# Softmax sums of a pooled-attention and feed-forward kernel: from a trip through DRAM to block transposes on VectorE

## The chip, the cores and the metric

The kernel runs on one core of a Trainium2 chip. The metric is the device time of one execution in microseconds, the median of several runs. TensorE (PE) does the products, VectorE (DVE) and ScalarE (ACT) the elementwise work, GpSimd (POOL) the reductions over partitions, and SyncE (SP) issues most of the transfers; SP's issues run in their program order, so one that waits holds up those behind it.

## The reference

```python
def _attn_ref(q, k, v):                       # 8 batches, 8 heads, 576 positions, 64 wide
    k_p = k.reshape(B, H, Sp, pool, D).mean(axis=3)      # pool 8: 72 keys
    v_p = v.reshape(B, H, Sp, pool, D).mean(axis=3)
    scores = scale * np.matmul(q, k_p.transpose(0, 1, 3, 2))
    scores = scores - np.max(scores, axis=-1, keepdims=True)
    attn = np.exp(scores)
    attn = attn / (np.sum(attn, axis=-1, keepdims=True) + 1e-09)
    return np.matmul(attn, v_p)
...
x = attn_out.transpose(0, 2, 1, 3).reshape(4608, 512)
h = np.maximum(x @ w_in, 0.0)                 # d_ff 2048
out = h * h @ w_out
```

The two weight matrices come as float64 and are turned to float32 on the chip.

## The kernel before

The 4608 tokens go in nine chunks (c) of 512. Of each chunk, 16 steps (fc) each make 128 of the 2048 hidden columns; step s = 16c + fc. `hidden` makes h with TensorE, ScalarE takes relu and square (r), `split_hidden` splits the result into a high part gh (ScalarE) and a rest gl (VectorE), and `project`, three steps later (LAG), multiplies both with the output weights w_o into four accumulators o: twelve products gh, gl, gh per step. In chunks 0 and 1 the products are plain (PLAIN = 2); from chunk 2 on `seven` makes two steps' h from seven products of half size per pair of steps, with sums of weight quarters (S1 to S4, tiles w_S) and of token halves (T1 to T4, B11 to B22, tiles x_T and x_B). An even step of it holds on VectorE the additions u, h, h (`soon`, behind a copy u by ScalarE) and one more h (`then`, behind another such copy). `x_sums` and `x_operand` make the x_T and x_B from xf: a subtraction xf, a copy by ScalarE for the high part, and a subtraction x_T or x_B on VectorE for the rest. T2 is the operand of the second product of a chunk.

The attention that a chunk needs is made in the steps ahead of it, by head pair (p = 0 to 3). For chunks from 2 on: `transpose_q` (qs, st), `scores` (sps on TensorE, sc on ScalarE, their maximum mx over partitions on GpSimd), `exponents` (ScalarE, and the sums tot over partitions on GpSimd, every row of tot the same), then the sums' reciprocals, and `weigh_values` (product av, times rb into xf on VectorE). Before, the sums went through DRAM: `send_sums` writes one row of each tot (rs), `fetch_sums` reads it as 128 x 8 (rc), `reciprocals` works on that (rr) and writes it (rd), and `fetch_reciprocals` reads it back, broadcast over 64 partitions (rb). A pair's first step is 16c - 23, -19, -15 or -11; the offsets of its stages from there stand in STEADY.

The order of all work is written out: a loop over the steps records each step's instructions, and a table `work`, filled by `at(step, f, ...)`, says which function is recorded in which step; inside a step the loop takes the kinds in a fixed order. Each engine then works through its instructions in that order. The output weights are turned to float32 in chunk 0 and 1, kept in DRAM, and fetched anew for each step (`fetch_weights`, w_o<-kept, 512 KB) into one of 40 buffers (SLOTS) that they share with the weights, x and xf tiles. k and v are summed in groups by transfers that add, issued by GpSimd (k<-in_k_dram). A weight is turned to float32 by `magnitude` (two activations on ScalarE, wf and raw) and `to_float32` (three operations on VectorE).

The tiles mx and tot share three buffers, rb, rr and qs have one, and the products sps, av, kps and pps share two PSUM buffers.

Of the kernel before, what the change touches and what calls it, by code (L numbers as in the profile page):

```python
# [37 lines left out]
def pooled_attn_relu2_ffn(  # L38
# [43 lines left out]

    STEADY = ((-23, -19, -15, -11), (-1, 1, 3, 5, 6, 6, 7, 8))
    EARLY = ((-13, -12, -9, -8), (0, 1, 2, 3, 4))
# [9 lines left out]
    kept = ctx.enter_context(tc.tile_pool(name="kept", bufs=1, space=bass.MemoryType.DRAM))  # L94
    dram = ctx.enter_context(tc.tile_pool(name="dram", bufs=3, space=bass.MemoryType.DRAM))
    ps_o = ctx.enter_context(tc.tile_pool(name="ps_o", bufs=1, space=bass.MemoryType.PSUM))
# [59 lines left out]

    def to_float32(*keys):
        parts = []
        for key in keys:
            words, m = raw.pop(key).rearrange("p a (n w) -> p a n w", w=2), wf[key]  # L160
            parts.append((words, m, m.bitcast(U32)))
        for _, m, _ in parts:
            DVE.tensor_scalar(m, m, EXP_MIN, EXP_MAX, op0=ALU.max, op1=ALU.min)
        for words, _, m in parts:
            DVE.scalar_tensor_tensor(m, m, 3, words[..., 0], op0=ALU.logical_shift_left, op1=ALU.bitwise_or)
        for words, _, m in parts:
            DVE.scalar_tensor_tensor(m, words[..., 1], 0x80000000, m, op0=ALU.bitwise_and, op1=ALU.bitwise_or)
# [235 lines left out]

    PER = 2 * CH // P

    def send_sums(c, p):
        sc, tots = live.pop((c, p))
        rs = dram.tile([2, CH], F32, name=f"rs_{c}_{p}", tag="rs")
        for i in range(2):
            dma(rs[i:i + 1], tots[i][0:1])  # L410
        live[c, p] = (sc, rs)

    def fetch_sums(c, p):
        sc, rs = live.pop((c, p))
        rc = sb.tile([P, PER], F32, name=f"rc_{c}_{p}", tag="rc", bufs=2)
        dma(rc, rs.rearrange("o (a f) -> (o a) f", f=PER))
        live[c, p] = (sc, rc)

    def reciprocals(c, p):
        sc, rc = live.pop((c, p))  # L420
        rr = sb.tile([P, PER], F32, name=f"rr_{c}_{p}", tag="rr", bufs=1)
        DVE.tensor_scalar(rr, rc, 1e-9, float(POOL), op0=ALU.add, op1=ALU.mult)
        DVE.reciprocal(rr, rr)
        rd = dram.tile([2, CH], F32, name=f"rd_{c}_{p}", tag="rd")
        dma(rd.rearrange("i (a f) -> (i a) f", f=PER), rr)
        live[c, p] = (sc, rd)

    def fetch_reciprocals(c, p):
        sc, rd = live.pop((c, p))
        rb = sb.tile([P, CH], F32, name=f"rb_{c}_{p}", tag="rb", bufs=1)  # L430
        for i in range(2):
            dma(rb[i * D:(i + 1) * D, :], rd[i:i + 1, :].broadcast_to([D, CH]))
        live[c, p] = (sc, rb)


# [211 lines left out]
    def project(c, fc):  # L647
# [12 lines left out]
        def store():  # L660
            for t in range(NTT):
                ob = half_tile("ob", f"ob_{c}_{t}")
                ACT.copy(ob, accs[c][t])
                rows = out[c * CH:(c + 1) * CH].rearrange("(p t) d -> t p d" if c == 0 else "(t p) d -> t p d", t=NTT)
                outs.append((rows[t], ob))
# [103 lines left out]
    weigh_values(0, 0)()  # L769
    to_float32(keys[0])  # L770
    token_turn(0, 2)()
    magnitude(keys[1])
    weigh_values(0, 1)()
    begin(0)
# [52 lines left out]
    START = {transpose_q: 9, scores: 12, exponents: 13}  # L827
    stages = (transpose_q, scores, exponents, send_sums, fetch_sums, reciprocals, fetch_reciprocals, weigh_values)
    for c in range(1, NCH):
# [10 lines left out]
        for p in range(NPAIR):  # L840
            s = c * NFC + first[p]
            at(s - 2 if c < PLAIN else max(s - QL, 8), load_q, c, p)
            for d, f in zip(offsets, names):
                at(max(s + d, START[f]) if c == PLAIN and f in START else s + d - (f is transpose_q and c >= PLAIN and p != 2), f, c, p)

# [4 lines left out]
    for s in range(-PRO, len(steps) + LAG):  # L850
        todo = work.get(s, [])
        soon, then, activate = hidden(*steps[s]) if 0 <= s < len(steps) else (None, None, None)
        later = [f(*a) for f, a in sorted(((f, a) for f, a in todo if f in on_pe), key=lambda x: x[0] is weigh_values)]
        for kind in (fetch_sums, fetch_weights):
            for f, a in todo:
                if f is kind:
                    f(*a)
        split_at(s, s - 2)
        if store:
# [17 lines left out]
        for f, a in todo:  # L877
            if f is fetch_reciprocals:
                f(*a)
        for f, a in todo:  # L880
            if f in first:
                f(*a)
        issue_loads()
        for f, a in todo:
            if f not in first + on_pe + last + (x_sums, x_operand, reciprocals, fetch_weights, fetch_sums, fetch_reciprocals, first_sums):
                f(*a)
# [48 lines left out]
```

## Time and profile before

| | us |
|---|---|
| median of 3 runs (lowest, highest) | 916.34 (914.07, 920.58) |
| profiled execution | 919.03 |
| its span | 917.3 |
| granted clock of TensorE, mean | 0.996 |
| busy: TensorE, VectorE, ScalarE, GpSimd | 897.3, 578.6, 511.2, 419.0 |

A row of a timeline has the start, the time and the engine of a run of like instructions (xN of them), and in brackets the idle time of the engine before the first and what ended it. A row of the groups has the busy time in all, and the mean of one in ns. A row of the waits has who waited for whom, the time in all, how many times, and the longest. A row of a table by stretches has the stretch, its length, the busy time of PE, PEld, DVE, ACT and POOL with the number of instructions in brackets, the granted clock as a share of the full one, the DMA engines' share and GB/s.

### The profile page before, as it was taken

How to read it: one execution, taken by the hardware profiler on the slowest of the kernel's cores; microseconds unless marked ns; L12 is line 12 of the kernel's file. 1: busy time of each engine (PE TensorE's matmuls, PEld its weight loads, DVE VectorE, ACT ScalarE, POOL GpSimd, SP SyncE). 2: the span in 40 equal slices, each digit the busy share in tenths (PEclk: the TensorE clock that was granted, in tenths of full speed). 3: DMA queues.
4: the chain of work that ended last, by engine and by line, in shares of the span. 5: the costliest groups of instructions: out<-in, count | busy, mean ns of one | idle time of the engine just before them, and what ended most of it. 6: DMA issues, size and time to landing. Idle time of an engine off the chain costs nothing.

```text
span 917.3 us, 14127 instructions
## 1 busy us (share of the span) xinstructions
PE 897.3 (98%) x5090; PEld 716.4 (78%) x5093; DVE 578.6 (63%) x941; ACT 511.2 (56%) x1018; POOL 419.0 (46%) x227
## 2 busy tenths in 40 slices
PE   8999999999999999999899999999999999999998
PEld 4344445677778888888788888888888888889987
DVE  7997679767788878666746485658544653353221
ACT  5776656656566655554654556545654564344343
POOL 4754136456655555556545656665444444200000
PEclk9999999999999999999999999999999999999999
DMA  9897564777556655766565557553534353345401
GB/s 222 252 266 189 136 149 114 227 216 203 144 134 165 142 141 139 174 145 140 111 174 147 134 130 188 140 137 99 184 100 123 100 168 111 127 142 202 185 1 47
DMA packets 157335, 138.72 MB, mean 151 GB/s; under 512 B 94488, under 2 KB 122136, under 8 KB 157264
## 3 DMA queue, kind: packets, MB, share of 16 engines
q1 hardware_dynamic: 128464, 127.13, 46.2%
q0 software_dynamic: 28800, 10.68, 10.2%
q8 instruction: 40, 0.66, 0.3%
q14 instruction: 31, 0.25, 0.1%
HBM read 119.65 MB, written 18.06 MB: 150 GB/s over the span
## 4 chain that ended last, share of the span: by engine, by line
PE 68%; DVE 10%; DMA 8%; issue 5%; ACT 4%; POOL 3%; SPq 1%; DVEq 0%; ACTq 0%; POOLq 0%
PE o L34 33%; PE h L34 30%; DMA w_o<-kept 3%; PE av L34 2%; PE sps L34 2%; DVE gl L34 1%; DVE wf_i L34 1%; DMA k<-in_k_dram 1%; DVE xf L34 1%; POOL tot L34 1%; ACT sc L34 1%; DMA rb<-rd 1%; DMA raw_i<-in_moe_w_in_dram 1%; POOL v L34 1%; ACT r L34 1%
## 5 line engine op out<-in xcount | busy, mean ns | idle before, releaser
L34 PE MATMUL o<-w_o,gh 128*128 128x512 f32 x1024 | 323.2, 397 | 4.4 <-DMA w_o<-kept 4.2
L34 POOL PARTITION_ALL_REDUCE tot<-sc x56 | 190.0, 3442 | 85.4 <-issue 81.2
L34 PEld LDWEIGHTS o<-w_o,gh 128*128 128x128 f32 x1024 | 185.0, 189 | 49.6 <-issue 6.3
L34 PE MATMUL o<-w_o,gl 128*128 128x512 f32 x512 | 201.5, 393 | 0.0
L34 ACT ACTIVATE r<-h 128x512 f32<-128x512 f32 x144 | 83.4, 594 | 91.2 <-PE h L34 74.0
L34 PE MATMUL h<-x_T,w_S 128*128 128x256 f32 x1008 | 130.4, 283 | 0.7 <-ACT x_T L34 0.4
L34 POOL PARTITION_ALL_REDUCE mx<-sc x56 | 109.9, 2002 | 40.3 <-ACT sc L34 29.1
L34 PEld LDWEIGHTS h<-x_T,w_S 128*128 128x128 f32 x1008 | 124.9, 190 | 1.1 <-ACT x_T L34 0.6
L34 PEld LDWEIGHTS o<-w_o,gl 128*128 128x128 f32 x512 | 96.5, 188 | 21.2 <-DVE gl L34 0.2
L34 DVE TENSOR_TENSOR h<-h,u 128x256 f32<-128x256 f32 x168 | 72.7, 433 | 60.1 <-ACT u L34 31.8
L34 ACT COPY u<-h 128x256 f32<-128x256 f32 x112 | 41.7, 372 | 121.9 <-PE h L34 75.1
L34 PE MATMUL h<-x_B,w_A 128*128 128x256 f32 x672 | 98.6, 283 | 0.5 <-ACT r L34 0.5
L34 DVE TENSOR_TENSOR gl<-r,gh 128x512 fp32r<-128x512 f32 x128 | 93.4, 765 | 6.0 <-ACT gh L34 5.9
L34 POOL DMA_DIRECT2D v<-in_v_dram x36 | 44.0, 1222 | 115.5 <-issue 39.6
L34 PEld LDWEIGHTS h<-x_B,w_A 128*128 128x128 f32 x672 | 91.7, 189 | 5.6 <-ACT r L34 0.9
L34 POOL DMA_DIRECT2D k<-in_k_dram x36 | 44.1, 1225 | 110.0 <-issue 53.0
L34 DVE TENSOR_TENSOR u<-h,u 128x256 f32<-128x256 f32 x56 | 23.3, 417 | 105.4 <-ACT u L34 105.3
L34 ACT ACTIVATE r<-r 128x512 f32<-128x512 f32 x144 | 84.2, 625 | 1.1
L34 DVE TENSOR_TENSOR st<-qs,st 64x512 fp32r<-64x512 f32 x56 | 46.3, 827 | 56.9 <-ACT st L34 56.0
L34 ACT CAST gh<-r 128x512 fp32r<-128x512 f32 x128 | 79.0, 617 | 0.9 <-PE o L34 0.7
L34 ACT ACTIVATE sc<-sc 72x512 f32<-72x512 f32 x56 | 34.5, 632 | 69.4 <-DVE sc L34 69.3
L34 PE MATMUL o<-wf_o,r 128*128 128x512 f32 x128 | 59.8, 611 | 0.0
(95 smaller groups left out, 1220.3 us busy)
## 6 DMA issues: line engine op xcount, KB each, us to landing
w_o<-kept SPq DMA_DIRECT2D x128, 512.0 KB
out_dram<-ob SPq DMA_DIRECT2D x36, 256.0 KB
raw_i<-in_moe_w_in_dram SPq DMA_DIRECT2D x16, 512.0 KB
raw_o<-in_moe_w_out_dram SPq DMA_DIRECT2D x16, 512.0 KB
kept<-w_o SPq DMA_DIRECT2D x16, 512.0 KB
rb<-rd SPq DMA_DIRECT2D x56, 128.0 KB
k<-in_k_dram POOLq DMA_DIRECT2D x36, 144.0 KB, 5.3
v<-in_v_dram POOLq DMA_DIRECT2D x36, 144.0 KB, 5.2
```

The costliest lines, as they stand in the source:

```text
L34: return lambda *a, **k: self.tc.keep_in_program_order(f(*a, **k))
```

## The change

1. `send_sums`, `fetch_sums` and `fetch_reciprocals` go. `turn_first` and `turn_second` transpose one tot each (64 x 512, in blocks of 32 x 32) into the halves of rb, so that each block's first column holds 32 tokens' sums; `reciprocals` works on those columns (128 x 16) into rr and transposes rr, broadcast along the block's columns, back into rb, where every row of a block then holds the reciprocals. `weigh_values` stays 8 steps behind a pair's first step.
2. In a step, turn_first is recorded ahead of `soon`, turn_second behind it, and reciprocals ahead of `x_sums` and `x_operand`.
3. From step 49 on a step's fetch of output weights is recorded at the end of the step before.
4. In the head, the first block of input weights is turned to float32 in two halves with `token_turn` recorded between, and the x_1 copy stands ahead of the next `magnitude`.
5. The first pair of chunk 1 is transposed a step earlier.
6. In a step, `token_normalise` and `late_turn_k` are recorded ahead of the other work of their group.
7. Two of the last chunk's four output copies are made by VectorE.

```diff
-    STEADY = ((-23, -19, -15, -11), (-1, 1, 3, 5, 6, 6, 7, 8))
+    STEADY = ((-23, -19, -15, -11), (-1, 1, 3, 5, 5, 5, 8))
...
-    def to_float32(*keys):
+    def to_float32(*keys, rows=slice(0, 2)):
...
-            words, m = raw.pop(key).rearrange("p a (n w) -> p a n w", w=2), wf[key]
+            words, m = raw[key].rearrange("p a (n w) -> p a n w", w=2)[:, rows], wf[key][:, rows]
...
+    def turn_first(c, p):
+
+        sc, tots = live[c, p]
+        rb = sb.tile([P, CH], F32, name=f"rb_{c}_{p}", tag="rb", bufs=1)
+        DVE.transpose(rb[:D, :], tots[0][:D, :])
+        live[c, p] = (sc, rb, tots[1])
+
+    def turn_second(c, p):
+        sc, rb, tot = live[c, p]
+        DVE.transpose(rb[D:, :], tot[:D, :])
+        live[c, p] = (sc, rb)
 
     def reciprocals(c, p):
...
+        rr = sb.tile([P, CH // SQ, 1], F32, name=f"rr_{c}_{p}", tag="rr", bufs=1)
+        DVE.tensor_scalar(rr, rb.rearrange("p (t w) -> p t w", w=SQ)[:, :, :1], 1e-9, float(POOL), op0=ALU.add, op1=ALU.mult)
         DVE.reciprocal(rr, rr)
...
+        DVE.transpose(rb.rearrange("p (t w) -> p t w", w=SQ), rr.broadcast_to([P, CH // SQ, SQ]))
...
-                ACT.copy(ob, accs[c][t])
+                (DVE.tensor_copy if c == NCH - 1 and t % 2 else ACT.copy)(ob, accs[c][t])
...
-    to_float32(keys[0])
+    to_float32(keys[0], rows=slice(0, 1))
     token_turn(0, 2)()
+    to_float32(keys[0], rows=slice(1, 2))
+    weigh_values(0, 1)()
     magnitude(keys[1])
-    weigh_values(0, 1)()
...
-                at(max(s + d, START[f]) if c == PLAIN and f in START else s + d - (f is transpose_q and c >= PLAIN and p != 2), f, c, p)
+                at(max(s + d, START[f]) if c == PLAIN and f in START else s + d - (f is transpose_q and (p != 2 if c >= PLAIN else p == 0)), f, c, p)
...
-        for kind in (fetch_sums, fetch_weights):
+        if s <= (PLAIN + 1) * NFC:
             for f, a in todo:
-                if f is kind:
+                if f is fetch_weights:
                     f(*a)
+        for f, a in todo:
+            if f is turn_first:
+                f(*a)
         split_at(s, s - 2)
...
         split_at(s, s - 1)
+        for f, a in todo:
+            if f is turn_second:
+                f(*a)
         for f in later:
             f()
...
+        for f, a in sorted(todo, key=lambda x: x[0] not in (token_normalise, late_turn_k)):
...
+        for f, a in work.get(s + 1, []):
+            if f is fetch_weights and s >= (PLAIN + 1) * NFC:
+                f(*a)
         while summed:
             summed.pop(0)()
-        for kind in (x_sums, x_operand, reciprocals, sum_of_quarters, first_sums):
+        for kind in (reciprocals, x_sums, x_operand, sum_of_quarters, first_sums):
```

On VectorE, in front of chunk 3 (steps 46 and 47; the first number behind a name is the pair or the hidden column block, the last one a running number), before:

```order
L34 TENSOR_TENSOR u_2_14_3228<-h_14_3202,u_2_14_3228 128x256
L34 TENSOR_TENSOR h_15_3203<-h_15_3203,u_2_14_3228 128x256
L34 TENSOR_TENSOR h_14_3202<-h_15_3203,u_2_14_3228 128x256
L34 TENSOR_TENSOR h_15_3203<-h_15_3203,u_2_14_3229 128x256
L34 TENSOR_TENSOR gl_12_3243<-r_12_3189,gh_12_3242 128x512
L34 TENSOR_TENSOR gl_13_3262<-r_13_3191,gh_13_3261 128x512
L34 TENSOR_TENSOR vp_2645<-v_4_1_2734 72x256
L34 TENSOR_TENSOR x_B_3280<-xf_1_2910,x_B_3280 128x512
L34 TENSOR_TENSOR x_T_3283<-xf_0_2336,x_T_3283 128x512
L34 TENSOR_TENSOR x_T_3286<-xf_0_2336,x_T_3286 128x512
L34 TENSOR_TENSOR xf_1_2910<-xf_1_2910,xf_0_2336 128x2x256
L34 TENSOR_TENSOR x_T_3333<-xf_1_2910,x_T_3333 128x512
```

With the change, step 46 first up to its second transpose (the xf of x_sums stands ahead of both extracts):

```order
L34 STREAM_TRANSPOSE rb_0_3195<-tot_0_0_3099 64x512
L34 TENSOR_TENSOR u_2_14_3181<-h_14_3155,u_2_14_3181 128x256
L34 TENSOR_TENSOR h_15_3156<-h_15_3156,u_2_14_3181 128x256
L34 TENSOR_TENSOR h_14_3155<-h_15_3156,u_2_14_3181 128x256
L34 STREAM_TRANSPOSE rb_0_3195<-tot_0_1_3100 64x512
```

and from there to the x_T of T2:

```order
L34 TENSOR_TENSOR h_15_3156<-h_15_3156,u_2_14_3182 128x256
L34 TENSOR_TENSOR gl_12_3198<-r_12_3142,gh_12_3197 128x512
L34 TENSOR_TENSOR gl_13_3217<-r_13_3144,gh_13_3216 128x512
L34 TENSOR_TENSOR vp_2610<-v_4_1_2703 72x256
L34 TENSOR_SCALAR rr_0_3233<-rb_0_3195 128x16
L34 RECIPROCAL rr_0_3233<-rr_0_3233 128x16
L34 STREAM_TRANSPOSE rb_0_3195<-rr_0_3233 128x512
L34 TENSOR_TENSOR x_B_3237<-xf_1_2869,x_B_3237 128x512
L34 TENSOR_TENSOR x_T_3240<-xf_0_2307,x_T_3240 128x512
L34 TENSOR_TENSOR x_T_3243<-xf_0_2307,x_T_3243 128x512
L34 TENSOR_TENSOR xf_1_2869<-xf_1_2869,xf_0_2307 128x2x256
L34 TENSOR_TENSOR x_T_3288<-xf_1_2869,x_T_3288 128x512
```

rb_0 is of pair 0 of chunk 4, which is turned while chunk 2 ends. Its first transpose moved in ahead of u and its second ahead of the last h, and the two small operations and the transpose back stand ahead of x_B, so that the x_T of T2 (the last row of each) stands five instructions further back; rr stood behind the x_T of T4 before.

In SP's queue, from the fetch for step 63 to that for step 65 (w_o_14 is that of chunk 3; rs_0 to rb_0 are of pair 0 of chunk 5), before:

```order
L34 DMA w_o_12_4314<-kept_1724 128x1024
L34 DMA rs_0_4351<-tot_0_0_4220 1x512
L34 DMA rs_0_4351<-tot_0_1_4221 1x512
L34 DMA k_6_1_4363<-in_k_dram 72x4x128
L34 DMA rc_0_4383<-rs_0_4351 128x8
L34 DMA w_o_13_4385<-kept_1809 128x1024
L34 DMA rd_0_4420<-rr_0_4417 128x8
L34 DMA w_o_14_4450<-kept_1866 128x1024
L34 DMA rb_0_4478<-rd_0_4420 64x512 x2
```

And with the change:

```order
L34 DMA w_o_12_4200<-kept_1715 128x1024
L34 DMA k_6_0_4205<-in_k_dram 72x4x128
L34 DMA w_o_13_4283<-kept_1792 128x1024
L34 DMA k_6_1_4298<-in_k_dram 72x4x128
L34 DMA w_o_14_4337<-kept_1849 128x1024
L34 DMA q_3_4404<-in_q_dram 32x10x32 x4
L34 DMA q_3_4404<-in_q_dram 32x6x32 x4
```

The transfers rs, rc, rd and rb are gone from between the fetches, and w_o_14 stands behind w_o_13 and a load of k with nothing of the softmax ahead of it.

On ScalarE, step 9 of chunk 0, the activations behind r_9, before:

```order
L34 ACTIVATE r_9_958<-r_9_958 128x512
L34 ACTIVATE wf_o_824<-raw_o_827 128x512
L34 ACTIVATE raw_o_827<-raw_o_827 128x512
L34 ACTIVATE wf_o_965<-raw_o_828 128x512
L34 ACTIVATE raw_o_828<-raw_o_828 128x512
L34 ACTIVATE kh_978<-kps_0_973 64x4x72 x4
```

And with the change:

```order
L34 ACTIVATE r_9_959<-r_9_959 128x512
L34 ACTIVATE kh_973<-kps_0_968 64x4x72 x4
L34 ACTIVATE wf_o_825<-raw_o_828 128x512
L34 ACTIVATE raw_o_828<-raw_o_828 128x512
L34 ACTIVATE wf_o_985<-raw_o_829 128x512
L34 ACTIVATE raw_o_829<-raw_o_829 128x512
```

The four kh, which the kl on VectorE take in, moved ahead of the four activations of two output weights.

More of the change, by code (lines that the diff above doesn't have):

```diff
@@ L94, in pooled_attn_relu2_ffn @@
     kept = ctx.enter_context(tc.tile_pool(name="kept", bufs=1, space=bass.MemoryType.DRAM))
-    dram = ctx.enter_context(tc.tile_pool(name="dram", bufs=3, space=bass.MemoryType.DRAM))
     ps_o = ctx.enter_context(tc.tile_pool(name="ps_o", bufs=1, space=bass.MemoryType.PSUM))
@@ L155, in magnitude @@
         ACT.activation(words[..., 0], halves[..., 1], AF.Copy, scale=LOW)
-    def to_float32(*keys):
+    def to_float32(*keys, rows=slice(0, 2)):
         parts = []
         for key in keys:
-            words, m = raw.pop(key).rearrange("p a (n w) -> p a n w", w=2), wf[key]
+            words, m = raw[key].rearrange("p a (n w) -> p a n w", w=2)[:, rows], wf[key][:, rows]
             parts.append((words, m, m.bitcast(U32)))
+            if rows.stop == 2:
+                raw.pop(key)
         for _, m, _ in parts:
@@ L401, in exponents @@
         live[c, p] = (sc, tots)
[L404 to L417, printed above, removed]
+    def turn_first(c, p):
[7 more added lines that the diff above has]
+        live[c, p] = (sc, rb)
     def reciprocals(c, p):
-        sc, rc = live.pop((c, p))
-        rr = sb.tile([P, PER], F32, name=f"rr_{c}_{p}", tag="rr", bufs=1)
-        DVE.tensor_scalar(rr, rc, 1e-9, float(POOL), op0=ALU.add, op1=ALU.mult)
+        sc, rb = live[c, p]
+        rr = sb.tile([P, CH // SQ, 1], F32, name=f"rr_{c}_{p}", tag="rr", bufs=1)
+        DVE.tensor_scalar(rr, rb.rearrange("p (t w) -> p t w", w=SQ)[:, :, :1], 1e-9, float(POOL), op0=ALU.add, op1=ALU.mult)
         DVE.reciprocal(rr, rr)
[L424 to L433, printed above, removed]
+        DVE.transpose(rb.rearrange("p (t w) -> p t w", w=SQ), rr.broadcast_to([P, CH // SQ, SQ]))
     def token_scores(c, p):
@@ L827, in pooled_attn_relu2_ffn @@
     START = {transpose_q: 9, scores: 12, exponents: 13}
-    stages = (transpose_q, scores, exponents, send_sums, fetch_sums, reciprocals, fetch_reciprocals, weigh_values)
+    stages = (transpose_q, scores, exponents, turn_first, turn_second, reciprocals, weigh_values)
     for c in range(1, NCH):
@@ L877, in pooled_attn_relu2_ffn @@
         for f, a in todo:
-            if f is fetch_reciprocals:
-                f(*a)
-        for f, a in todo:
             if f in first:
@@ L883, in pooled_attn_relu2_ffn @@
         issue_loads()
-        for f, a in todo:
-            if f not in first + on_pe + last + (x_sums, x_operand, reciprocals, fetch_weights, fetch_sums, fetch_reciprocals, first_sums):
+        for f, a in sorted(todo, key=lambda x: x[0] not in (token_normalise, late_turn_k)):
+            if f not in first + on_pe + last + (x_sums, x_operand, turn_first, turn_second, reciprocals, fetch_weights, first_sums):
                 f(*a)
```

## The prediction

> **What bounds the kernel now.** I read the page first: busy shares, then the chain that ended last.
>
> ```profile
> PE 897.3 (98%) x5090; PEld 716.4 (78%) x5093; DVE 578.6 (63%) x941; ACT 511.2 (56%) x1018; POOL 419.0 (46%) x227
> ...
> PE 68%; DVE 10%; DMA 8%; issue 5%; ACT 4%; POOL 3%; SPq 1%; DVEq 0%; ACTq 0%; POOLq 0%
> ```
>
> TensorE is busy for 897.3 of 917.3 us, and the change leaves its instructions and their order alone. So everything that can be won lies in 20 us of gaps, and everything that can be lost is a new gap. The second view is therefore what TensorE waited for.
>
> ```profile
> PE o L34 <- DMA w_o<-kept: 4.2, 4, 2.4
> PE pps L34 <- DVE kl L34: 2.1, 1, 2.1
> PE sps L34 <- DVE xf L34: 1.9, 2, 1.0
> ```
>
> Four waits on the fetched output weights (4.2 us in all, the longest 2.4) and one on VectorE's kl (2.1 us) are the largest that the change touches. Third, since the change moves work from DMA queues to VectorE, I looked for places where VectorE has nothing to spare, by stretches of 24 us.
>
> ```profile
> 240.00:264.00 24.00, 23.95 (x132) 19.92 (x131) 19.68 (x31) 11.74 (x22) 11.92 (x8) 1.00 0.49 116
> 264.00:288.00 24.00, 22.61 (x145) 19.54 (x144) 20.50 (x32) 16.95 (x34) 13.45 (x8) 1.00 0.62 171
> 288.00:312.00 24.00, 24.00 (x155) 21.12 (x154) 21.07 (x33) 13.95 (x29) 12.35 (x7) 1.00 0.58 140
> 312.00:336.00 24.00, 23.65 (x149) 20.55 (x149) 18.07 (x27) 15.95 (x31) 13.96 (x7) 1.00 0.55 129
> ```
>
> The fourth column is VectorE. In chunk 2 (256 to 333 us) it works 18 to 21 of 24 us, against 63% over the span: here, and in front of each later chunk's first product, an instruction more on VectorE can reach TensorE. Elsewhere it has some 9 us free in 24.
>
> **What the turns cost on VectorE.** Twenty-eight head pairs get three transposes, a tensor_scalar and a reciprocal each.
>
> ```profile
> L34 DVE STREAM_TRANSPOSE qs<-q 128x512 f32<-128x512 f32 x28 | 19.6, 701 | 0.0
> L34 DVE RECIPROCAL rr<-rr 128x8 f32<-128x8 f32 x28 | 5.7, 203 | 1.0
> L34 DVE TENSOR_SCALAR rr<-rc 128x8 f32<-128x8 f32 x28 | 5.0, 179 | 0.4
> L34 DVE STREAM_TRANSPOSE still<-still 128x32 f32<-128x32 f32 x1 | 0.2, 211 | 0.0
> ```
>
> The 128x512 transpose is in the trace: 0.70 us. From 0.21 us at 32 columns to 0.70 at 512 its time goes by the columns (0.49 us for 480). No row shows 64 partitions: bounded between half (0.35) and whole (0.70), I take 0.70, since the columns set the time. The two small ones grow from 8 to 16 columns and stay near 0.18 and 0.20. Sum per pair: 3 x 0.70 + 0.38 = 2.48 us, where 0.38 stood before; so +2.1 us per pair and 28 x 2.1 = +59 us on VectorE, 579 to about 638. The DMA trip that goes (rs, rc, rd, rb) was never itself what TensorE waited for, so its removal is worth only what it clears for others.
>
> GpSimd is summing the next pair while VectorE turns. Whether that stretches a transpose is open.
>
> ```profile
> L34 DVE TENSOR_TENSOR xf<-xf,xf 128x512 f32<-128x512 f32 x14 | 20.3, 1452 | 0.2
> L34 DVE TENSOR_TENSOR xf<-av,rb 128x512 f32<-128x512 f32 x28 | 19.3, 689 | 31.1 <-PE av L34 25.9 <-DMA rb<-rd 2.9 <-DMA q<-in_q_dram 1.8
> ```
>
> The form with both inputs in SBUF takes 1452 ns in the mean, the form with one in PSUM 689; the 28 transposes stay at a mean of 701. I take no stretching; a transpose stretched as the first row would add 0.75 us to each. The Trainium skill, "SBUF — State Buffer", section "Who interferes with whom", says that an operation of VectorE with at most one SBUF input does not contend with GpSimd outside the two-port modes; by that rule nothing is added, and the trace's rows agree for the 128-partition transposes, while no row shows it for the new ones. Were the rule wrong here, the sum below would be about 5 us higher.
>
> **The head (parts 4 to 6).** Three stalls are edited.
>
> ```profile
> 28.13 1.10 PE L34 MATMUL h<-x,wf_i 128*128 128x512 f32 x2 [1.44 <-ACT x L34]
> 54.14 1.07 PE L34 MATMUL sps<-kf,st 64*64 64x72 f32 x18 [1.10 <-DVE st L34]
> ...
> 94.79 0.42 DVE L34 TENSOR_TENSOR kq<-k 72x256 f32<-72x256 f32 x1 [1.93 <-DMA k<-in_k_dram]
> ...
> 101.54 0.65 ACT L34 ACTIVATE wf_o<-raw_o 128x512 f32<-128x512 f32 x1
> ...
> 105.42 1.86 DVE L34 SCALAR_TENSOR_TENSOR kl<-kps,kh 64x288 fp32r<-64x288 f32 x4 [4.51 <-ACT kh L34]
> 107.43 0.86 PE L34 MATMUL pps<-ident,te 128*72 128x128 f32 x4 [2.08 <-DVE kl L34]
> 108.00:112.00 4.00, 4.00 (x8) 1.80 (x7) 3.25 (x7) 3.86 (x7) 1.19 (x1) 0.62 0.33 37
> ```
>
> The first two stalls, 1.44 and 1.10 us, should shrink, since the first half of the weights is done before the second is begun and the transpose no longer stands behind the wf_o block. But at 94.79 VectorE waits 1.93 us for the last addition of k, whose transfers GpSimd issues, and the kps transposes at 101 hang on it: TensorE 2.5 us earlier at 54 would wait there instead. I count nothing for the first two (bound: 2.5 us, if those transfers also move up). The third counts: kh goes ahead of four activations that begin at 101.54 and last 2.2 us, so kl ends 2.2 us earlier and the idle 2.08 us goes. Behind it the granted clock was 0.62 over 4 us, worth (1 - 0.62) x 4 = 1.5 us, which I take to go with the idle. **Head: -3.6 us**, bounds -1 and -6.
>
> The Trainium skill, "TensorE: Matmul & The Clock Gate", section "What's actually happening", lets the clock halve after an idle window of about 3.4 us. By that, idle times of 2.08 us here and 2.43 us below would cost no clock, 2.9 us less would be gained, and the sum below would give 918.6. The trace does not agree: 0.62 stands right behind 2.08 us of idle, so I keep the trace's price.
>
> **The weight fetches (part 3).** In the queue of SP, fetch w_o_14 stood behind rd, which waits for VectorE's rr; now it is issued a step earlier and rd is gone.
>
> ```profile
> 448.67 0.32 SPq L34 DMA_DIRECT2D rd<-rr  x1
> 449.08 0.39 SPq L34 DMA_DIRECT2D w_o<-kept  x1
> ...
> 456.32 1.22 PE L34 MATMUL o<-w_o,gh 128*128 128x512 f32 x2 [2.43 <-DMA w_o<-kept]
> ...
> 460.51 0.88 PE L34 MATMUL h<-x_B,w_A 128*128 128x256 f32 x6
> ...
> 551.81 0.73 PE L34 MATMUL o<-w_o,gh 128*128 128x512 f32 x2 [0.59 <-DMA w_o<-kept]
> ...
> 634.00 0.62 PE L34 MATMUL o<-w_o,gh 128*128 128x512 f32 x2
> ...
> 636.75 0.88 PE L34 MATMUL h<-x_B,w_A 128*128 128x256 f32 x6
> ```
>
> At 456 TensorE idles 2.43 us, and the twelve o products behind it take 460.51 - 456.32 = 4.19 us, where a project step elsewhere takes 636.75 - 634.00 = 2.75: 1.44 us of lowered clock. With the 0.59 at 551.81 that is 4.46 us. The other two waits (4.2 - 2.43 - 0.59 = 1.2 us together) are in chunks 1 and 2, where the issue's place is unchanged or the tile's buffer comes free late; they stay. **Fetches: -4.5 us**, bounds -2 (the landing stays as slow as the 7 us here) and -5.7.
>
> **Chunk 2, where VectorE is full.** Four pairs turn there: 4 x 2.1 = 8.4 us more against 24 - 19.68, 24 - 20.50, 24 - 21.07 and 24 - 18.07, together 16.7 us free in 96. Part of the free time is the wait between two additions, which recurs in each even step:
>
> ```profile
> 345.41 0.43 DVE L34 TENSOR_TENSOR h<-h,u 128x256 f32<-128x256 f32 x1 [0.44 <-ACT u L34]
> ```
>
> turn_second now stands exactly in that 0.44 us, so 4 x 0.44 = 1.8 of the 8.4 us are covered. Of the other 6.6 some falls into stretches in which VectorE waits for TensorE, at the end of 312 to 336 above all. Bounds 0 and +6.6; I take **+2.5 us**, nearer the lower end, as TensorE in 312:336 has 23.65 of 24 us of its own work and VectorE 5.9 us free there.
>
> **Front of each chunk.** The pair that turns at step 16c - 2 puts turn_first, turn_second and the reciprocals ahead of the chain gl, vp, x_B, x_T, xf, x_T that makes T2, needed by the second product of the chunk. Three transposes from start to start about 0.62 each, 0.35 for the small ones, less the 0.44 that is covered: 1.8 us later.
>
> ```profile
> 351.31 0.69 DVE L34 TENSOR_TENSOR x_T<-xf,x_T 128x512 fp32r<-128x512 f32 x1 [0.69 <-ACT x_T L34]
> ...
> 352.05 2.30 PE L34 MATMUL h<-x_T,w_S 128*128 128x256 f32 x17 [0.34 <-DVE x_T L34]
> ...
> 444.61 0.69 DVE L34 TENSOR_TENSOR x_T<-xf,x_T 128x512 fp32r<-128x512 f32 x1 [0.99 <-ACT x_T L34]
> ...
> 445.64 1.60 PE L34 MATMUL h<-x_T,w_S 128*128 128x256 f32 x12
> ...
> 636.81 0.69 DVE L34 TENSOR_TENSOR x_T<-xf,x_T 128x512 fp32r<-128x512 f32 x1 [0.69 <-ACT x_T L34]
> ...
> 637.46 2.38 PE L34 MATMUL h<-x_T,w_S 128*128 128x256 f32 x18
> ```
>
> At chunk 3 TensorE already waits for it: +1.8. At chunk 6 x_T ends at 637.50 and is used at 637.46: no slack, +1.8. At chunk 4 it ends at 445.30 and is needed at 445.64 (0.34), and VectorE waited 0.99 there instead of 0.69 (0.30): 1.8 - 0.64 = +1.1, of which I take 0.7 as the waits ahead of it close too; the same for chunk 5, where I found the same slack. Chunks 7 and 8 have more room. **Fronts: +5.0 us**, bounds 0 and +9 (with all six at 1.5).
>
> The store's copies on VectorE (part 7) run beside the last o products: 0.
>
> **Sum**: -3.6 - 4.5 + 2.5 + 5.0 = -0.6 us. The profiled execution took 919.03 us (span 917.3), so it would be 918.4; the median of the runs is 916.34, 2.7 lower, and the same difference gives 915.7.
>
> **Rivals.** (a) The turns are hidden: fronts and chunk 2 cost at most 1 us. For it: VectorE's waits between those rows (0.99, 0.69, 0.44) can close, and 59 us stand against 339 us idle. Against: the slacks at chunks 3 and 6. Then -8.1 + 1 = -7, or down to -11 with the head's whole bound: 905 to 909. (b) Slower: the front of chunks 3 to 6 becomes VectorE-bound, and each new stall, 0.7 (0.35 + 0.34) + 1.8 = 2.5 us at chunk 3, passes the length (2.1 us) behind which the clock was lowered; four fronts at 1.8 + 1.45 = 13 and chunk 2 at +6.6, less 8.1, is +11.5: 928. It decides from stalls of about 2 us upward; for it the 2.08 and 2.43 us rows, against it that 1.44 us at 28 is shorter than that and was followed by the ordinary 1.10 for two products. (c) The wait for GpSimd takes the place of the DMA's.
>
> ```profile
> 361.67 6.86 POOL L34 PARTITION_ALL_REDUCE tot<-sc  x2
> ...
> 365.50 0.41 DVE L34 TENSOR_TENSOR u<-h,u 128x256 f32<-128x256 f32 x1
> ```
>
> Here the second tot ends at 368.53, and turn_second, estimated at 1.5 us behind u at 365.50, would wait 1.5 us, with h, gl and what follows queued behind it. TensorE needs gl two steps on, with about 2.5 us of cover, so one such wait costs nothing; were the cover 1 us, 0.6 us for each of some eight pairs, +5: 921. (d) The fetches wait for buffers rather than for rd, so part 3 does nothing: +4.5 - 0.6 = +3.9: 920.
>
> **Chances.** The forecast with (c) and (d), which stay within 1%, 0.74; (a) as far as below 907.2, 0.15; (b) above 925.5, 0.11. One per cent, 9.2 us, is about what a measurement of this kernel can tell from no change. The range runs from 907 to 923: the lower end is the sum with fronts and chunk 2 near nothing, the upper one the sum with fronts and chunk 2 at +4 more each; about a tenth is left out on either side.
>
> **What would show it.** Right: no TensorE wait on kl near 105, and clock 1.0 behind it; w_o<-kept waits of about 1.2 us; x_T waits grown from 0.7 us to 5 or so; VectorE near 638 us; transposes of 64x512 at 0.70 us. Wrong: transposes at half or twice that; long waits of VectorE on tot; TensorE waiting for h or gl in the middle of chunks; the clock row below 1.0 at chunk fronts.

## The result and the profile after

The changed kernel took 922.41 us (median of 9 runs, 919.55 to 928.57) against 919.48 us before (9 runs, 914.07 to 921.41) on the same chip: a ratio of 1.0056, 95% interval 1.0034 to 1.0078. A second comparison gave 922.54 against 920.10 us, 1.0034 (1.0008 to 1.0060). So by the ratios it is 3 to 5 us slower; the time lay inside the range, but 0.6 us less had been forecast, and the sign is wrong. The profiled execution, 928.08 us with a span of 925.9, stands at the slow end of these runs, so some of its waits may be larger than usual; a second profile of the same kernel (e4 below) took 920.19 us, span 918.0.

The page of the changed kernel, busy times and the chain that ended last:

```profile
PE 900.0 (97%) x5090; PEld 719.3 (78%) x5093; DVE 642.5 (69%) x1030; ACT 510.3 (55%) x1016; POOL 409.9 (44%) x227
...
PE 65%; DVE 12%; issue 7%; DMA 5%; ACT 4%; POOL 4%; SPq 0%; DVEq 0%; ACTq 0%; POOLq 0%
```

VectorE gained 63.9 us (578.6 to 642.5; 59 were forecast) and two points of the chain. What TensorE waited for, in the changed kernel:

```profile
PE kps L34 <- DVE tm L34: 5.8, 1, 5.8
PE sps L34 <- DVE xf L34: 3.0, 2, 1.6
PE h L34 <- ACT r L34: 2.2, 1, 2.2
PE o L34 <- DMA w_o<-kept: 1.9, 1, 1.9
...
PE h L34 <- DVE x_T L34: 1.5, 5, 0.3
...
PE h L34 <- DVE h L34: 0.7, 1, 0.7
```

The wait on kl is gone and those on w_o fell from 4.2 to 1.9 us, as forecast; new are 5.8 us for tm and 0.7 for h, and the wait for r grew from 0.5 to 2.2 us. The five waits for x_T are the fronts of the later chunks: 0.3 us each.

The groups of the new VectorE work:

```profile
L34 DVE STREAM_TRANSPOSE rb<-tot 64x512 f32<-64x512 f32 x56 | 39.3, 703 | 28.9 <-POOL tot L34 27.7
L34 DVE STREAM_TRANSPOSE rb<-rr 128x512 f32<-128x512 f32 x28 | 19.9, 711 | 1.0
L34 DVE TENSOR_SCALAR rr<-rb 128x16 f32<-128x16 f32 x28 | 9.0, 320 | 0.0
L34 DVE RECIPROCAL rr<-rr 128x16 f32<-128x16 f32 x28 | 7.1, 253 | 1.0
```

Sixty-four partitions take as long as 128 (703 and 711 ns). Per pair that is 39.3 / 28 + (19.9 + 9.0 + 7.1) / 28 = 2.69 us, where 2.48 was forecast: the two small operations took 0.32 and 0.25 us, not 0.18 and 0.20. No transpose is stretched beside GpSimd: the 84 of the pairs took 694 to 714 ns. The Trainium skill, "SBUF — State Buffer", section "Who interferes with whom", says that an operation of VectorE with at most one SBUF input, outside the two-port modes, does not contend with GpSimd, and the trace agrees for these transposes.

Where TensorE lost and won, in the timelines. At 106 us:

```profile
101.54 0.42 DVE L34 TENSOR_TENSOR kq<-k 72x256 f32<-72x256 f32 x1 [6.40 <-DMA k<-in_k_dram]
...
106.45 0.74 PE L34 MATMUL kps<-ident,kq 72*128 72x72 f32 x4 [5.81 <-DVE tm L34]
...
90.90 1.19 POOL L34 DMA_DIRECT2D k<-in_k_dram  x1 [9.05 <-issue]
95.01 1.20 POOL L34 DMA_DIRECT2D k<-in_k_dram  x1 [2.92 <-issue]
```

The last k transfer is issued at 95.01; VectorE waits for it 6.40 us in front of wf_o and tm, and tm frees the buffer that kps needs. In the first profile of before, the same transfer was issued at 90.94. At the front of chunk 2, on VectorE, ScalarE and TensorE:

```profile
249.43 1.44 DVE L34 STREAM_TRANSPOSE rb<-tot 64x512 f32<-64x512 f32 x2
250.90 0.69 DVE L34 TENSOR_TENSOR w_S<-wf_i,w_S 128x512 fp32r<-128x512 f32 x1
251.51 1.62 DVE L34 TENSOR_TENSOR gl<-r,gh 128x512 fp32r<-128x512 f32 x1
...
253.87 0.71 DVE L34 STREAM_TRANSPOSE rb<-rr 128x512 f32<-128x512 f32 x1
...
259.88 0.68 DVE L34 TENSOR_TENSOR gl<-r,gh 128x512 fp32r<-128x512 f32 x1
...
260.66 0.60 ACT L34 ACTIVATE r<-h 128x512 f32<-128x512 f32 x1 [2.18 <-DVE gl L34]
...
261.31 2.75 PE L34 MATMUL h<-x_T,w_S 128*128 128x256 f32 x12 [2.15 <-ACT r L34]
```

The pair's three transposes and two small operations stand in VectorE's row ahead of gl; gl frees r, r frees h, and TensorE stands 2.15 us. Before, TensorE ran the same matmul at 255.28 without a wait, inside this run of 18:

```profile
254.56 2.32 PE L34 MATMUL h<-x_T,w_S 128*128 128x256 f32 x18
```

At 305 to 316 us, on SP and TensorE:

```profile
308.75 0.31 SPq L34 DMA_DIRECT2D v<-in_v_dram  x1
309.15 0.95 SPq L34 DMA_DIRECT2D w_o<-kept  x2
...
315.72 0.88 PE L34 MATMUL o<-w_o,gh 128*128 128x512 f32 x2 [1.91 <-DMA w_o<-kept]
```

Two fetches are issued together behind a load of v, and the first lands 6.5 us later. At 465.43 the matmul that had waited 2.43 us in the first profile of before waits no longer.

### The profile page after: what moved, and what is told of

It reads as the page before. It is cut to its first block, busy times and chain, and to the rows that moved or that the text cites. A ratio compares the mean times of both kernels' runs of the same rounds, so it can differ in the third digit from the quotient of the medians.

```text
span 925.9 us, 13921 instructions
## 1 busy us (share of the span) xinstructions
PE 900.0 (97%) x5090; PEld 719.3 (78%) x5093; DVE 642.5 (69%) x1030; ACT 510.3 (55%) x1016; POOL 409.9 (44%) x227
## 4 chain that ended last, share of the span: by engine, by line
PE 65%; DVE 12%; issue 7%; DMA 5%; ACT 4%; POOL 4%; SPq 0%; DVEq 0%; ACTq 0%; POOLq 0%
PE o L34 31%; PE h L34 29%; PE av L34 3%; DVE gl L34 2%; PE sps L34 2%; POOL tot L34 2%; DMA w_o<-kept 2%; DVE wf_i L34 2%; DMA k<-in_k_dram 2%; DMA q<-in_q_dram 1%; DVE xf L34 1%; ACT r L34 1%; DVE w_S L34 1%; DVE x_T L34 1%; ACT sc L34 1%
## 5 line engine op out<-in xcount | busy, mean ns | idle before, releaser
L34 PE MATMUL h<-x_T,w_S 128*128 128x256 f32 x1008 | 132.7, 286 | 4.1 <-ACT r L34 2.2
L34 POOL PARTITION_ALL_REDUCE mx<-sc x56 | 102.1, 1871 | 40.3 <-ACT sc L34 40.3
L34 DVE TENSOR_TENSOR gl<-r,gh 128x512 fp32r<-128x512 f32 x128 | 104.5, 853 | 5.9 <-ACT gh L34 5.2
L34 DVE TENSOR_TENSOR st<-qs,st 64x512 fp32r<-64x512 f32 x56 | 48.6, 867 | 29.0 <-ACT st L34 28.2
L34 PE MATMUL h<-x,wf_i 128*128 128x512 f32 x128 | 59.9, 614 | 0.8 <-DVE wf_i L34 0.8
```

The source lines that it names most:

```text
L34: return lambda *a, **k: self.tc.keep_in_program_order(f(*a, **k))
```

## The experiments

All times stand beside runs of the kernel before on the same chip.

**e1, the head alone.** Before, with parts 4 to 7.

```diff
+    to_float32(keys[0], rows=slice(0, 1)) ... rows=slice(1, 2)     # parts 4, 5, 6, 7
     stages = (..., send_sums, fetch_sums, reciprocals, fetch_reciprocals, weigh_values)   # as before
```

> The kernel before with parts 4 to 7 alone (weights turned in halves, earlier transpose, kh ahead, copies of the store); the sums still go through DRAM. Theory A (the head's edits gain, and the 5.8 us TensorE wait for tm at 106 in the changed kernel came from GpSimd's k transfers, which land late in some executions whatever the kernel): no wait on kl near 105, time 2 to 4 us below before. Theory B (the edits themselves push the k transfers late): the wait for tm of some 5 us stands at 101 to 107 in this profile too, and the time is 2 to 5 us above before.

918.64 against 920.10 us, 0.9988 (0.9956 to 1.0019): no difference that can be told. TensorE's wait for tm stands in its profile with 7.4 us, the one for kl is gone, and, unexpected, the 2.43 us wait at 456 is gone too, though neither turns nor fetches were changed. Neither theory's time came out.

**e2, the turns alone.** Parts 1 to 3 on the head of before.

```diff
-    to_float32(keys[0], rows=slice(0, 1)) ...                       # parts 4 to 7 undone
     stages = (transpose_q, scores, exponents, turn_first, turn_second, reciprocals, weigh_values)
```

> The changed kernel with the head of before (parts 1 to 3 alone). Theory A (chunk 2 is VectorE-bound: the turns put 2.3 us in front of chunk 2 and 3.4 us near 306, each with 1.5 us of lowered clock, and the fetches give back 1.3 us at 195 and 3.8 us at 456): these steps of the delay stand in this profile as in the changed kernel's, and the time is 2 to 4 us above before. Rival (the head made the whole loss): no TensorE wait over 1 us between 250 and 320, time 3 to 5 us below before.

927.18 against 920.10 us, 1.0078 (1.0048 to 1.0109). Parts 1 to 3 and not the head carry the loss, and more of it than theory A had (7.2 us against 2 to 4). Waits for xf, r and w_o stand between 220 and 320 us; its fetch at 310.92 is again two behind a load of v.

**e3, DRAM trip for the pairs of chunks 2 and 3.**

```diff
+        if PLAIN <= c < 4:
+            names, offsets = trip, (-1, 1, 3, 5, 6, 6, 7, 8)
```

> The changed kernel, but the pairs of chunks 2 and 3 (made while chunks 1 and 2 run) send their sums through DRAM as before; block transposes from the pairs of chunk 4 on. Theory A (the loss lies in chunk 2, where VectorE is full): the waits at 255 and 306 to 316 and their lowered clock go, 6 to 9 us below the changed kernel, and 3 to 6 us below before. Rival (the loss is spread over the fronts of all chunks): 1 to 2 us below the changed kernel.

919.77 against 920.10 us, 0.9995 (0.9971 to 1.0020), 2.8 us below the changed kernel in the same comparison (e4). The waits at 255 and 305 went, as theory A said, but the gain is half of what it said. Its profile loses nothing in chunk 2: against e6 (the comparison is explained behind e15) it is 5.6 us late at 219.7 us and at 309.4 us. Its wait for tm in the head was 7.1 us; whether the head took the rest of the gain in the other executions is not shown.

**e4, the changed kernel again.**

> The changed kernel once more, unedited, for a second profile and its time beside the other three. Theory A (the wait for tm at 106 is chance of the transfers): it is absent or of another length, the waits at 255 and 306 to 316 are there again within 0.5 us. Theory B (the head's edits make it): it stands again at 5 to 6 us.

922.54 against 920.10 us, 1.0034 (1.0008 to 1.0060). The wait for tm was 2.2 us instead of 5.8: its length is chance of the execution. The wait for r at the front of chunk 2 was there again, 2.23 us; the one of 1.9 us for w_o was not.

**e5, before again.**

> The kernel before once more, unedited, for a second profile of it. Theory A (the 2.43 us wait for w_o at 456 and its lowered clock, which went in every profile since, even where the fetches were not moved, were chance of the one execution): no wait for w_o over 1.2 us, and TensorE's starts from 460 on some 4 us earlier against its own 450 than in the first profile. Rival (it belongs to the kernel before): a wait of 2 to 2.5 us at the same matmul.

919.02 us; this is the profile that decides two terms of the forecast. TensorE and GpSimd in it:

```profile
455.71 0.50 PE L34 MATMUL o<-w_o,gh 128*128 128x512 f32 x1
...
78.92 1.20 POOL L34 DMA_DIRECT2D k<-in_k_dram  x1 [3.58 <-issue]
89.00 1.19 POOL L34 DMA_DIRECT2D k<-in_k_dram  x1 [8.88 <-issue]
```

No wait at 455.71, where the first profile had 2.43 us and 1.44 us of lowered clock: that stall was chance. And the third k transfer has 8.88 us of idle time ahead of it by GpSimd's row. In the first profile of before it was this:

```profile
86.91 1.19 POOL L34 DMA_DIRECT2D k<-in_k_dram  x1 [5.34 <-issue]
```

In the fifteen profiles read beside the first one it is 7.0 to 9.1 us: the forecast's profile was the exception. In e5 the kernel before waits 1.7 us for tm and 3.4 us for kl.

**e6, the head without part 5.**

```diff
-    s + d - (f is transpose_q and (p != 2 if c >= PLAIN else p == 0))
+    s + d - (f is transpose_q and c >= PLAIN and p != 2)
```

> The kernel before with parts 4, 6 and 7, without part 5 (the first pair of chunk 1 is transposed where it was). Theory A (part 5 frees the q buffer a step earlier, so eight q transfers go ahead of the raw weights in SP's queue, these land at 85 to 90 us instead, and GpSimd's third k transfer takes 9 to 10 us instead of 6.5): the third and fourth k transfers are issued at 86 to 87 and 91 again, no wait for tm at kps, 3 to 5 us below before. Rival (part 4 or 6 does it): the wait for tm of 2 to 7 us is there, and the time is within 2 us of before.

917.01 against 919.72 us, 0.9970 (0.9952 to 0.9988): parts 4, 6 and 7 gain 2.8 us. The mechanism in the expectation fell all the same: the third k transfer was issued at 87.91, with 8.84 us of idle time ahead of it, though part 5 is gone. The wait for tm was 1.8 us.

**e7, the early fetches alone.**

```diff
+        for f, a in work.get(s + 1, []):
+            if f is fetch_weights and s >= (PLAIN + 1) * NFC:        # sums through DRAM
```

> The kernel before with part 3 alone (fetches recorded a step earlier from step 49 on, the sums through DRAM). Theory A (the fetches' waits were worth about 1 us in a usual execution): within 2 us of before. Rival (the forecast's term): 4 to 5 us below before, waits for w_o under 1.3 us in all.

919.02 against 919.72 us, 0.9989 (0.9968 to 1.0010): theory A. The waits for w_o come to 1.7 us, against 2.3 in e5.

**e8, one pair through DRAM.**

```diff
-            for d, f in zip(offsets, names):
+            for d, f in zip(TRIP, trip) if c == 3 and p == 0 else zip(offsets, names):
```

> The changed kernel, but pair 0 of chunk 3 alone (turned in step 30, ahead of chunk 2's first operands and of the gl that frees r) goes through DRAM. Theory A (that pair's 2.5 us on VectorE make the 2.2 us wait for r at 255 to 261 and the lowered clock behind it): this wait goes, the later ones stay, 3 to 4 us below the changed kernel (918 to 919.5 if that gives 922.5). Rival (any of the pairs fills VectorE as much): the wait shrinks by under 1 us or moves, time within 1.5 us of the changed kernel.

921.22 against 919.72 us, 1.0001 (0.9976 to 1.0025), against 1.0034 for the changed kernel in the other comparison: 3.0 us less by the ratios, but 0.9 us by the medians (1.5 against 2.4 us above before), with intervals that overlap, so the times do not decide between the two. The profile says more. The wait for r fell from 2.2 to 1.1 us, and from 219.7 us to the sps at 271 TensorE loses 0.7 us against e6, where the profiles with all turns lose 2.5 to 3.1 (table behind e15). The wait for w_o near 311 was there with 2.0 us. One pair of 28 is a large part of the loss, not the whole of it.

**e9, the changed kernel without part 5** (the diff of e6 on the changed kernel).

> The changed kernel with part 5 alone undone. Theory A (part 5 makes the wait of kps for tm longer: 2.2 to 7.4 us in the five profiles with it, 0 to 3.0 in the five without): wait for tm of 0 to 3 us, 2 to 4 us below the changed kernel, so about level with before. Rival (the wait's length is chance, and the difference of the profiles too): no change against the changed kernel.

923.78 against 920.04 us, 1.0034 (1.0012 to 1.0057), the same ratio as the changed kernel in e4. The wait for tm was 2.9 us. So part 5 costs nothing that the runs can tell; with e1 against e6 (0.9988, 0.9970, intervals that overlap) its effect stays open. For the turns this run is the clean partner of e12 and e15, which lack parts 1 and 2 alone.

**e10, v a step later.**

```diff
-    KV_AT = (("k", -35), ("v", -27))
+    KV_AT = (("k", -35), ("v", -26))
```

> The changed kernel with the loads and additions of v one step later (KV_AT of v from -27 to -26). Theory A (near 306 SP's queue holds a load of v that waits for VectorE's kq, and behind it the fetch of w_o that TensorE waits 1.9 us for): the load no longer waits there, the wait for w_o and its lowered clock near 306 to 320 go, 2 to 4 us below the changed kernel. Rival (the fetch waits for its own buffer or for bandwidth): the wait stays within 0.5 us.

(`turn_k` keeps its step.) 936.07 against 920.04 us, 1.0168 (1.0123 to 1.0212): slower. The order of GpSimd's transfers and sums moves too, and TensorE's waits move to other fetches and to h:

```profile
PE o L34 <- DMA w_o<-kept: 7.6, 3, 2.9
PE h L34 <- DVE h L34: 6.2, 12, 1.1
```

It tells nothing on the fetch at 309: whether that is late because of the load of v stays open.

**e11, turns from the pairs of chunk 4 on, without part 5** (the diffs of e3 and e6 on the changed kernel).

> Parts 1 to 4, 6 and 7, with block transposes only for the pairs of chunks 4 to 8, and without part 5. Theory A (turns cost nothing once VectorE has room, part 5 costs 2 to 4 us): 2 to 5 us below before. If the turns also gain where they are: below the next run by over 1 us; if they cost at the fronts of chunks 3 to 7 (0.4 us each in the delay against before): above it by 1 to 2 us.

917.42 against 920.04 us, 0.9969 (0.9948 to 0.9990): 6 us below e9.

**e12, parts 3, 4, 6 and 7, no turns.**

> Parts 3, 4, 6 and 7 alone: no turns at all, the sums through DRAM, no part 5. Theory A: the run without part 5 and with neither turns nor early fetches was 2.8 us below before, early fetches alone 1 us below; together 3 to 4 us below before. Rival (the early fetches collide with the transfers of the sums): no better than 2.8 us below.

915.60 against 920.04 us, 0.9931 (0.9900 to 0.9961), 9.5 us below e9. Its profile is of an execution of 926.44 us, which lost 10 us against e6 ahead of 194.7; from 219.7 to 309.4 it loses 0.1 us.

**e13, the turns a step later.**

```diff
-    STEADY = ((-23, -19, -15, -11), (-1, 1, 3, 5, 5, 5, 8))
+    STEADY = ((-23, -19, -15, -11), (-1, 1, 3, 6, 6, 6, 8))
```

> The changed kernel without part 5, with the turns and reciprocals at offset 6 instead of 5 (they then fall in odd steps, two steps ahead of weigh_values instead of three). Theory C (VectorE's waits for GpSimd's tot, 28 to 40 us in the profiles, hold up gl and h and cost TensorE): these waits fall under 5 us and the time falls 3 to 7 us below the run without part 5. Theory A (they stand where VectorE is idle anyway; what costs is VectorE's 2.5 us per pair in chunks 1 to 3): the waits fall and the time stays within 2 us.

932.73 against 920.68 us, 1.0134 (1.0101 to 1.0168). VectorE's waits for tot, 35.4 us in e9, are gone altogether, and the kernel is some 9 us slower than e9. What theory C forecast did not come, nor did theory A's time. That the waits are free is not shown by this run alone, since the same work now stands at another place. But between 200 and 330 us, where the loss falls, VectorE waits for tot 0.0 us in the changed kernel, 1.2 in e4 and 1.2 in e9: those waits stand elsewhere. The largest new waits are in the chains of x_T and of w_A:

```profile
PE h L34 <- ACT x_T L34: 4.8, 5, 3.2
PE h L34 <- DVE w_A L34: 3.5, 1, 3.5
```

**e14, short turns.** The same for the second transpose and tot; `reciprocals` then reads 16 columns of that block. The kernel leaves out the sums of all other columns, so its weights are not the softmax's.

```diff
-        DVE.transpose(rb[:D, :], tots[0][:D, :])
+        DVE.transpose(rb[:D, :SQ], tots[0][:D, :SQ])
```

> The changed kernel without part 5, with the two transposes of the sums cut to their first 32 columns (64x32 instead of 64x512; the reciprocals then work on columns of that block, so the weights are not the softmax's): the same instructions, order and waits, 2 x 0.49 = 1.0 us less VectorE per pair, 27 us in all. Theory A (VectorE's time in chunks 1 to 3 is the price): 2 to 4 us below the run without part 5. Theory C (waits and order are the price): within 1 us of it.

923.01 against 920.68 us, 1.0016 (0.9991 to 1.0041), 1.7 us below e9's ratio, between the figures of the two theories and with intervals that overlap. In the profiles it is clearer. VectorE's page line of e9 and of e14:

```profile
PE 898.1 (97%) x5093; PEld 716.0 (78%) x5093; DVE 638.2 (69%) x1030; ACT 511.1 (55%) x1016; POOL 410.4 (44%) x227
```

```profile
PE 897.1 (98%) x5090; PEld 715.6 (78%) x5093; DVE 619.4 (67%) x1030; ACT 510.7 (56%) x1016; POOL 410.8 (45%) x227
```

TensorE's matmul at the front of chunk 2, in e9 and in e14:

```profile
258.09 1.10 PE L34 MATMUL h<-x_T,w_S 128*128 128x256 f32 x7 [2.15 <-ACT r L34]
```

```profile
255.29 0.98 PE L34 MATMUL h<-x_T,w_S 128*128 128x256 f32 x6 [1.22 <-ACT r L34]
```

Some 1.0 us less transposing per pair (18.8 us less VectorE in all, since other operations took longer), 0.9 us less wait for TensorE there. The waits for tot stayed (29.8 us).

**e15, no turns again.**

> Parts 3, 4, 6 and 7 alone once more, for a second profile and time (the first profile was of a disturbed execution). Theory A (no turns is better than turns from chunk 4 on, which cost 1.2 to 2.3 us at the front of chunk 3 and 0.7 at that of chunk 4): 3 to 6 us below before, no wait for x_T above 0.4 us, delay against the run without part 5 between -2 and 0 us from 460 on. Rival (the 0.9931 was luck of the executions): within 0.2 per cent of 0.997.

916.06 against 920.68 us, 0.9952 (0.9924 to 0.9979). With e12 this is the fastest version, 4 to 6 us below before and, by the ratios, 7.5 to 9.5 us below e4 and e9.

The delay of TensorE tells where each version loses: the start of the same matmul in its trace, less its start in that of e6 (us). The places are a matmul of chunk 1, the sps at 220, the front of chunk 2, the sps at 271, one behind the fetch at 305, the project behind the front of chunk 3, the front of chunk 4, and two projects and a front later on. Only the change from column to column counts: the first one holds what the head did in that execution.

| start in e6 | 194.7 | 219.7 | 254.6 | 270.6 | 309.4 | 353.2 | 444.5 | 460.7 | 548.7 | 728.8 |
|---|---|---|---|---|---|---|---|---|---|---|
| changed kernel | 3.9 | 5.0 | 6.8 | 7.5 | 12.2 | 12.1 | 12.7 | 11.4 | 10.8 | 10.8 |
| e4, the same again | -0.8 | -1.0 | 1.4 | 2.1 | 4.1 | 4.2 | 4.8 | 3.5 | 2.8 | 2.9 |
| e8, one pair through DRAM | 2.1 | 3.3 | 3.9 | 3.9 | 6.5 | 6.2 | 6.8 | 5.4 | 4.9 | 4.9 |
| e9, all turns, no part 5 | 0.3 | 1.8 | 3.5 | 4.8 | 6.8 | 8.5 | 9.2 | 7.9 | 7.2 | 7.3 |
| e14, short turns | -0.2 | -0.1 | 0.7 | 1.6 | 2.7 | 3.2 | 3.8 | 2.5 | 1.8 | 1.9 |
| e11, turns from chunk 4 | -0.5 | 0.2 | 0.4 | 0.4 | 0.4 | 2.6 | 3.3 | 2.0 | 1.3 | 1.4 |
| e15, no turns | -1.0 | -0.5 | -0.5 | -0.5 | -0.5 | 0.5 | 0.6 | -0.4 | -1.6 | -2.5 |

From 219.7 to 309.4 us, in chunk 2, the three profiles with all turns lose 7.2, 5.1 and 5.0 us, e8 3.2, e14 2.7, and the two in which that chunk turns nothing 0.2 and 0.0. Less VectorE time at the same places nearly halves the loss; VectorE's time is the price.

## Why the prediction was wrong, step by step

Gains and costs can be set against the runs as two sums. The forecast had -8.1 us of gains (head and fetches) and +7.5 us of costs (chunk 2 and fronts). Parts 3, 4, 6 and 7 alone measured -6.3 and -4.4 us by the ratios (e12, e15), and e9, which adds the turns, stands 9.5 and 7.5 us above these. So the gains were too high by 2 to 4 us, and that alone turns the sign. The costs came out at or above their sum by luck, since chunk 2 was put too low and the fronts too high.

**The gains were read from one execution.** This is the step that failed first. "Fetches: -4.5 us" took the 2.43 us wait at 456 and the 1.44 us of clock behind it as a property of the kernel. No other profile has them at that matmul, e5's of the same kernel neither. The early fetches measured 1.0 us (0.9989) alone; beside the head's edits 1.7 and 3.6 us (e15 and e12 against e6), and 1.5 us in the delays of e15 from 195 to 729. Each is a small difference against intervals of some 2 us, and none reaches 4.5.

**The head.** Forecast -3.6 us; parts 4, 6 and 7 measured -2.8 us (0.9970). The sign and the mechanism held: the wait for kl, 2.08 us in the first profile of before and 3.4 in the second, is gone in the changed kernel's first profile and 1.1 us in its second. The limit that the forecast named, the transfers of k, was there as well, and it was worse than the profile showed: the usual idle time ahead of the third is 7.0 to 9.1 us, not 5.34, and the wait for tm, absent in the first profile, was 0.5 to 7.4 us in all others but one.

**Chunk 2.** The term that was mis-sized. "I take +2.5 us" within bounds of 0 and 6.6, since VectorE had room late in the chunk; 5.0 to 7.2 us were lost between 220 and 309. The room was not where it was needed. Of the loss 2.5 to 3.1 us fall before the sps at 271, and most of that goes to the pair that turns ahead of chunk 2 (the row at 249.43): with this pair through DRAM (e8) only 0.7 us is lost there. The fronts of the forecast begin with chunk 3, so this pair was priced as VectorE time alone, against the 4.3 us free in 240:264; and a front was followed along VectorE's row to T2, not to gl, which frees r, which frees h. Behind 271 another 2.0 to 4.7 us are lost: near 305, u and h come 0.7 us late, and in the changed kernel's first profile the fetch behind the load of v 1.9. The whole loss came before 312, in windows whose busy shares had been read as nearly full, and VectorE's free time from 312 to 336 did not pay it back: from 309 to 340 the delays fall by 0.5 to 1.6 us, but those of the two profiles of before by 0.8 and 1.0 as well.

**Fronts.** Forecast +5.0 us for chunks 3 to 6. Behind 309.4 us the changed kernel's delay moves by -1.4, e4's by -1.2 and e9's by +0.5 us, where e15, with no turns, moves by -2.0: the turns cost 0.7, 0.9 and 2.5 us there in all. Front by front, by the same delays just ahead of and just behind each front, less those of e15, and the same in all three profiles: chunk 4 costs 0.7 us and chunk 5 0.6, near the 0.7 forecast; chunk 7, forecast at nothing, 0.5; and chunk 6, forecast at 1.8, 0.5 to 0.6. Chunk 3 differs between them, 0.5 to 1.9, where 1.8 was forecast. The waits for x_T, forecast to grow to some 5 us, come to 1.9 (1.5 and 0.4). At chunk 6, in the changed kernel:

```profile
631.72 2.85 DVE L34 TENSOR_TENSOR xf<-xf,xf 128x512 f32<-128x512 f32 x1
...
644.90 0.69 DVE L34 TENSOR_TENSOR x_T<-xf,x_T 128x512 fp32r<-128x512 f32 x1 [0.69 <-ACT x_T L34]
...
645.65 2.29 PE L34 MATMUL h<-x_T,w_S 128*128 128x256 f32 x17 [0.27 <-DVE x_T L34]
```

From that xf to the x_T of T2 it now takes 644.90 - 631.72 = 13.2 us; before, from the start of this row to the x_T at 636.81, it took 636.81 - 626.29 = 10.5:

```profile
626.29 2.85 DVE L34 TENSOR_TENSOR xf<-xf,xf 128x512 f32<-128x512 f32 x1
```

So the chain did become longer, by 2.7 us, where 1.8 had been estimated. But it also began earlier against TensorE, 645.09 - 631.72 = 13.4 us ahead of the first product with T2 (645.09 by TensorE's row) instead of 637.46 - 626.29 = 11.2, and 0.27 us of wait is left: the forecast had held the rest of VectorE's row fixed against TensorE's.

**The sum again with what was measured**: head -2.8, fetches -1.0 to -3.6, chunk 2 +5.0 to +7.2, fronts +0.7 to +2.5: between -1 and +6 us, where the runs say +3 to +5. Rival (a), hidden turns, falls with the 7.5 to 9.5 us between e9 and the runs without turns. Rival (b) had the direction, VectorE as the bound with a lowered clock behind the new stalls, but the largest stalls stand in chunk 2 and not at the fronts of chunks 3 to 6, and the clock fell in some executions only. Rivals (c) and (d) came nearest in time, 921 and 920, but not by their mechanisms as far as is shown. (c) was real in size, 27.7 us of VectorE's waits for tot, but at most 1.2 us of these waits stand where the loss falls. Of (d) it holds that the early fetches bring little (e7); that they wait for buffers is not shown. The bounds held for the head and the fronts. The fetches' -1.0 and -1.7 lie short of their bound of -2, and the 7.2 us in chunk 2 lie above 6.6; within the bounds, the choice was too favourable for the fetches and for chunk 2.

**The clock.** Three profiles have nearly the same idle time ahead of the same matmul at the front of chunk 2: 2.15 us in the changed kernel, 2.23 in e4 and 2.15 in e9. The stretches behind them, in this order:

```profile
261.00:265.00 4.00, 3.69 (x15) 3.50 (x16) 2.09 (x5) 3.22 (x7) 1.21 (x1) 0.57 0.68 208
```

```profile
256.00:260.00 4.00, 4.00 (x15) 3.71 (x16) 2.20 (x5) 2.94 (x6) 1.21 (x1) 0.50 0.72 214
```

```profile
258.00:262.00 4.00, 3.91 (x23) 3.50 (x24) 2.10 (x5) 3.01 (x7) 1.21 (x1) 1.00 0.71 196
```

Granted were 0.57, 0.50 and 1.00. Four us on in e6's time, the three have lost 3.3, 5.3 and 1.7 us since 219.7. But what follows evens this out. The sps at 271 needs VectorE's xf; in the same order:

```profile
278.16 0.31 PE L34 MATMUL sps<-st,kl 128*72 128x192 f32 x1 [1.40 <-DVE xf L34]
```

```profile
272.68 0.31 PE L34 MATMUL sps<-st,kl 128*72 128x192 f32 x1
```

```profile
275.43 0.31 PE L34 MATMUL sps<-st,kl 128*72 128x192 f32 x1 [2.46 <-DVE xf L34]
```

Behind these the loss since 219.7 is 2.5, 3.1 and 3.0 us. With the full clock TensorE waits longest for VectorE. So whether a stall of about 2.2 us lowers the clock was not decided by its length, as rival (b) had it, but differs by execution; and at this place the lowered clock made no more than 0.6 us of difference in the end, since TensorE otherwise waits for VectorE. The Trainium skill, "TensorE: Matmul & The Clock Gate", section "What's actually happening", says that the window of about 3.4 us runs freely and isn't started by the kernel; that agrees with one length giving both outcomes, though its full idle window isn't what these rows show, since 2.15 and 2.23 us sufficed.

## What to carry to other kernels

A gain that rests on one wait of a shared transfer has to be seen in a second profile before it enters a sum: of the two gains forecast here one was a stall that no other profile showed at its place, and the other lay beside a transfer that was early in that execution alone. Where work moves from transfers that nobody waits for to an engine, price it at every front by the chains in which that engine frees a buffer for the bottleneck (gl to r to h), and not by its free time in a stretch; the trip through DRAM here was hidden from TensorE, and the fastest version keeps it (0.9931 and 0.9952) with the head's edits and the early fetches.

## What was not expected of the hardware

The tensor_scalar on the 16 sums of a partition, with one input in SBUF, took 158 to 1025 ns in the changed kernel (mean 320); before, on 8 sums, 164 to 480 (mean 179). What stretches it no run shows. Beside it the transposes back into rb kept to 711 to 714 ns. And a 64x512 transpose takes the 0.70 us of a 128x512 one, 64x32 (e14) takes 0.20: its time goes by the columns.
